# A routed mixture-of-experts kernel on one core: TensorE's branches, its flags, and the place of one transposition in the step

## The chip, the cores and the metric

The kernel runs on one core of a Trainium2 chip. Five engines work beside each other, each through its own list of instructions in the order of the program: TensorE (PE, matrix products; PEld are its weight loads), VectorE (DVE), ScalarE (ACT), GpSimd (POOL) and SyncE (SP, which here issues the loads of weights). They wait for one another by semaphores. The metric is the device time in microseconds (us) of one execution; the time of a kernel is the median of its runs.

## The reference

Attention with a sigmoid, a two-layer network with PReLU, and then a mixture of eight experts of which each token takes one. The change lies in the last part alone:

```python
logits = x @ w_gate                      # 1792 tokens x 768, 8 experts
expert_idx = np.argmax(logits, axis=1)
gate_w = probs[np.arange(N), expert_idx]
for e in range(E):
    xe = x[expert_idx == e]
    h = np.maximum(xe @ w1[e], 0.0)      # 768 x 1024
    ye = h @ w2[e]                       # 1024 x 768
    out[mask] = gate_w[mask, None] * ye
```

All is float32. Each factor of a product is split into a high part that TensorE takes exactly and a low rest, and three products are summed: hi x hi, hi x lo and lo x hi (the "rests").

## The kernel before

**Blocks.** The tokens of an expert are gathered into blocks of 128 slots. There can be 21 of them (TMAX); how many there are, which expert each has and which tokens, is found on the chip. Here 17 blocks run, 0 to 16. Steps 1 to 13 are laid out one behind the other; from there on a chain of branches (tail) asks before each step whether there is another block. A block with 64 tokens or fewer is "half full": its low parts are put into the free slots 64 to 127 of the high tile, so the hi products do the rests too, and the rests are skipped. Here blocks 2, 12 and 13 are half full. Each engine learns that by itself: hold(b) loads slot 64 of the block's list into a register of PE, ACT and DVE, and full(b) compares it with the number of tiles NT.

**Work of one block b.** tx(b) turns the gathered tokens xg (from block 3 on on DVE: L784, into xt; ACT copies xt into bh, L785; DVE makes the rest bl, L786). moe1(b) on PE: 24 hi products of bh with the high (L797) and low (L798) parts of w1, then 12 rests of bl (L806) behind a branch (L810). ACT copies the sum into hr (L814). th(b): eight 128x128 transpositions of hr on PE (L840), then hh on ACT and hl on DVE. moe2(b) on PE: 32 hi products (L894, L895) and 16 rests (L897). out_rows(b) scales the rows on DVE (ye, L911; a half-full block also uses ACT), and POOL scatters them.

**The step.** The whole program is recorded in the order in which the code is run (a manual schedule): no scheduler moves anything. step(b) runs: out_rows and scatter of block b-2; the split of w2 for block b-1, if its expert is new (ACT L700, DVE L701, eight pieces each), and the next load of w2 on SP; moe1(b); the gathers for block b+2 on POOL; tx(b+1); the split of w1 for block b+1, if its expert is new (ACT L679, DVE L681 and L684), and the next load of w1; moe2(b-1), with th(b) put in ahead of its last two rounds of products. So every engine finds work of three blocks in its list. moe1(1) has tx(2), and moe1(2) has th(1), at a place between: behind its hi products. Experts change at blocks 3, 4, 6, 13 and 14: w2 is split in steps 4, 5, 7, 14 and 15, w1 in steps 2, 3, 5, 12 and 13.

**Places.** In the trace of before, moe1(4) starts on PE at about 683 us of the span, moe1(5) at 701, moe1(6) at 719, moe1(9) at 771, moe1(13) at 840, moe1(14) at 855, moe1(15) at 872.

Of the kernel before, what the change touches and what calls it, by code (L numbers as in the profile page):

```python
# [20 lines left out]
ACT = mybir.EngineType.Activation  # L21
DVE = mybir.EngineType.DVE
PE = mybir.EngineType.PE
# [3 lines left out]
def kernel(ctx, tc, kq, v, w_in, w_out, alpha, w_gate, w1, w2, out):  # L27
# [13 lines left out]
    nc = tc.nc  # L41
    P = 128
# [4 lines left out]
    NT, DM = out.shape  # L47
    HP = DM // P
    NF = w_in.shape[0]
    E, _, _, F2 = w1.shape  # L50
    K2 = F2 // P
    HN = DM // 2
    NTT = NT // P
    TMAX = (NT + E * (P - 1)) // P
# [354 lines left out]
    rt = {}  # L409
# [233 lines left out]
    ex = {}  # L643
# [101 lines left out]
    def ps2(key, name):  # L745

        if "fix" not in ex:
            return psum2(name)
        if key not in fixed:
            fixed[key] = psum2(f"f{key}")  # L750
        return fixed[key]

    H = P // 2
    HALF = 2
    held = {}

    def full(b):

        return held[b] < NT

    def hold(b):
        if b >= HALF:
            held[b] = nc.values_load(rt["ids"][H:H + 1, b:b + 1], engines=[PE, ACT, DVE], min_val=0, max_val=2 * 4096)

    def tx(b):

        xg = ex["xg"][b % 4]
        bh, bl = ex["bx"][b % 2]
        hold(b)
        if b < 3:  # L770
            pt = ps2("x", f"tx{b}")
            for k in range(HP):
                nc.tensor.transpose(pt[:, k // 4, (k % 4) * P:(k % 4 + 1) * P], xg.rearrange("p (r k) -> p k r", k=HP)[:, k, :], ident)
            parts = [(pt[:, z, :n * P].rearrange("p (k m) -> p k m", k=n), slice(4 * z, 4 * z + n)) for z, n in ((0, 4), (1, 2))]
            for src, d in parts:
                nc.scalar.activation(bh[:, d, :], src, AF.Copy)
            for src, d in parts:
                nc.vector.tensor_tensor(bl[:, d, :], src, bh[:, d, :].bitcast(F32), ALU.subtract)
        else:

            if "xt" not in ex:
                ex["xt"] = main.tile([P, HP, P], F32, tag="raw", bufs=2, name="xt")
            t = ex["xt"]
            nc.vector.transpose(t.rearrange("p k (q s) -> p k q s", q=G), xg.rearrange("p (q i k) -> p k q i", q=G, k=HP))  # L784
            nc.scalar.activation(bh, t, AF.Copy)  # L785
            nc.vector.tensor_tensor(bl, t, bh.bitcast(F32), ALU.subtract)  # L786
        if b >= HALF:
            with tc.If(held[b] >= NT):  # L788
                nc.vector.tensor_copy(bh[:, :, H:], bl[:, :, :H].bitcast(F32))

    def moe1(b, between=None):
        bh, bl = ex["bx"][b % 2]
        pt = ps2("2" if b == 1 else "1", f"e1_{b}")
        for k in range(HP):
            _, _, h, l = ex["w1"][k]
            for n in range(2):
                nc.tensor.matmul(pt[:, n, :], bh[:, k, :], h[n], start=(k == 0), stop=False)  # L797
                nc.tensor.matmul(pt[:, n, :], bh[:, k, :], l[n], start=False, stop=(b >= HALF and k == HP - 1))  # L798
        if between:
            between()  # L800

        def rests():
            for k in range(HP):
                h = ex["w1"][k][2]
                for n in range(2):
                    nc.tensor.matmul(pt[:, n, :], bl[:, k, :], h[n], start=False, stop=(k == HP - 1), skip_group_check=b >= HALF)  # L806
        if b < HALF:
            rests()
        else:
            with tc.If(full(b)):  # L810
                rests()
        if b == 1:
            next_split(1, 2)
        nc.scalar.activation(ex["hr"], pt, AF.Relu if b < HALF else AF.Copy)  # L814
# [15 lines left out]
    def turn(b, n):  # L830

        if "fix" not in ex:
            pt = psum1(f"th{b}_{n}")
        else:
            if f"t{n}" not in fixed:
                fixed[f"t{n}"] = psum1(f"ft{n}")
            pt = fixed[f"t{n}"]
        for k in range(4):
            sl = slice(k * P, (k + 1) * P)
            nc.tensor.transpose(pt[:, sl], ex["hr"][:, n, sl], ident)  # L840
        return pt

    def turned(b, n, pt):
        hh, hl = ex["hh"][b % 2][:, n, :], ex["hl"][b % 2][:, n, :]
        nc.scalar.activation(hh, pt, AF.Copy)
        nc.vector.tensor_tensor(hl, pt, hh.bitcast(F32), ALU.subtract)
# [20 lines left out]
    def th(b, halves=(0, 1)):  # L867
        if b < HALF:
            for n in halves:
                turned(b, n, turn(b, n))  # L870
        else:
            turned_pair(b, [turn(b, n) for n in range(2)])
# [14 lines left out]
    def moe2_mm(b, pt, k, n, parts="hl", end=False):  # L887

        ks = slice((k % 4) * P, (k % 4 + 1) * P)
        a, c = (ex[x][b % 2][:, k // 4, ks] for x in ("hh", "hl"))  # L890
        h, l = ex["w2"][k]
        ns = slice(n * HN, (n + 1) * HN)
        if "h" in parts:
            nc.tensor.matmul(pt[:, n, :HN], a, h[:, ns], start=(k == 0), stop=False)  # L894
            nc.tensor.matmul(pt[:, n, :HN], a, l[:, ns], start=False, stop=end)  # L895
        if "l" in parts:
            nc.tensor.matmul(pt[:, n, :HN], c, h[:, ns], start=False, stop=(k == K2 - 1), skip_group_check=b >= HALF)  # L897

# [23 lines left out]
    def moe2(b, between):  # L922
        pt = ps2("2", f"e2_{b}")
        for k in range(K2):
            if k == K2 - 2:
                between()
            for n in range(2):
                moe2_mm(b, pt, k, n, "h", b >= HALF and k == K2 - 1)

        def rests():  # L930
            for k in range(K2):
                for n in range(2):
                    moe2_mm(b, pt, k, n, "l")
        if b < HALF:
            rests()
        else:
            with tc.If(full(b)):
                rests()

        def store():  # L940
            out_rows(b, ex["y"][b % 2].rearrange("p (a n) -> p a n", a=2), pt[:, :, :HN])
            scatter(b)
        ex["store"] = store

    def stored():
        ex.pop("store", lambda: None)()
# [14 lines left out]
    def moe2_last(b):  # L961

        next_split(2, b)
        stored()
        hh, hl = ex["hh"][b % 2], ex["hl"][b % 2]
        y = ex["y"][b % 2]
        TH = DM // 3
        for n, (c0, c1) in enumerate(((0, 2 * TH), (2 * TH, DM))):
            pt = ps2("1x"[n], f"e2_{b}_{n}")[:, 0, :]
            for k in range(K2):  # L970
                ks = slice((k % 4) * P, (k % 4 + 1) * P)
                x = hh[:, k // 4, ks]
                h, l = (w[:, c0:c1] for w in ex["w2"][k])
                nc.tensor.matmul(pt[:, :c1 - c0], x, h, start=(k == 0), stop=False)
                nc.tensor.matmul(pt[:, :c1 - c0], x, l, start=False, stop=(k == K2 - 1))
            with tc.If(full(b)):
                for k in range(K2):
                    xl, h = hl[:, k // 4, (k % 4) * P:(k % 4 + 1) * P], ex["w2"][k][0][:, c0:c1]
                    nc.tensor.matmul(pt[:, :c1 - c0], xl, h, start=False, stop=(k == K2 - 1), skip_group_check=True)
            out_rows(b, y[:, c0:c1], pt[:, :c1 - c0])  # L980
            for z in range(c0 // TH, c1 // TH):
                scatter(b, z)
# [13 lines left out]
    def next_split(which, b):  # L996
        if b < TMAX:
            c = (nc.values_load(rt["row0"][0:1, 2:3], engines=[ACT, DVE], min_val=0, max_val=1)
                 if (which, b) == (1, 1) else changed(b, [ACT, DVE]))
            with tc.If(c > 0):  # L1000
                for k in range(HP if which == 1 else K2):
                    (split_w1 if which == 1 else split_w2)(k)

    def second_weights(b):
        next_split(2, b)
        next_w(2, b + 1)

    def step(b, s2=None):
        for _ in s2 or ():
            pass  # L1010
        stored()
        if b > 1:
            second_weights(b - 1)
        moe1(b, {1: lambda: tx(2), 2: lambda: th(1)}.get(b))
        gate_of(b)
        if b + 2 < TMAX:
            gather(b + 2)
        if 1 < b < TMAX - 1:
            tx(b + 1)
        if b > 1:  # L1020
            next_split(1, b + 1)
        next_w(1, b + 2)
        if b > 1:
            moe2(b - 1, lambda: th(b))
# [18 lines left out]
    with tc.manual_schedule():  # L1043
# [12 lines left out]
        c0, c1 = NCH - 2, NCH - 1  # L1056
# [87 lines left out]
        pt = turn(0, 1)  # L1144
# [82 lines left out]
```

## Time and profile before

| | before |
|---|---|
| median of 3 runs | 935.57 us (935.48 to 935.58) |
| the profiled execution | 930.77 us |
| its span in the profile | 929.0 us |
| mean granted clock of TensorE in it | 0.993 of full speed |
| PE busy | 907.8 us, 98% of the span |
| DVE, ACT busy | 566.3 us (61%), 346.4 us (37%) |
| mixture of experts | about 640 to 929 us of the span |

The profile is of one execution. Times in it count from the start of its span. Its summary gives the busy time of each engine and its share; a list of waits says for each engine which producer's instruction ended its idle time ("PE f L894 <- ACT hr L814" is: PE, about to run line 894, waited for ACT's write of hr in line 814); a name with q (DVEq, PEldq) is the engine's instruction queue, as against its arithmetic. A timeline gives single instructions or runs of them with start and length, and in brackets the idle time ahead of the first with what ended it. The granted clock is the share of full speed (2.4 GHz) that TensorE was given; 0.50 is 1.2 GHz.

### The profile page before, as it was taken

How to read it: one execution, taken by the hardware profiler on the slowest of the kernel's cores; microseconds unless marked ns; L12 is line 12 of the kernel's file. 1: busy time of each engine (PE TensorE's matmuls, PEld its weight loads, DVE VectorE, ACT ScalarE, POOL GpSimd, SP SyncE). 2: the span in 40 equal slices, each digit the busy share in tenths (PEclk: the TensorE clock that was granted, in tenths of full speed). 3: DMA queues.
4: the chain of work that ended last, by engine and by line, in shares of the span. 5: the costliest groups of instructions: out<-in, count | busy, mean ns of one | idle time of the engine just before them, and what ended most of it. 6: DMA issues, size and time to landing. Idle time of an engine off the chain costs nothing. (4 is left out here: it accounts for less than half of the span.)

```text
span 929.0 us, 14602 instructions
## 1 busy us (share of the span) xinstructions
PE 907.8 (98%) x5367; PEld 753.6 (81%) x5367; DVE 566.3 (61%) x1017; ACT 346.4 (37%) x543; POOL 137.9 (15%) x149
## 2 busy tenths in 40 slices
PE   9999999999999999999999999999999999999895
PEld 3333348989999899998999899988888899888795
DVE  2765534467777677776777644685588632247831
ACT  6666642222232222322223232343476421144710
POOL 0000000000000000000000000137254442433531
PEclk9999999999999999999999999999999999999898
DMA  7665500011121111211112021451667511148400
GB/s 274 189 202 177 182 1 1 1 52 52 52 68 52 52 52 52 69 52 52 52 52 68 18 85 53 154 238 47 248 248 291 186 52 35 44 171 306 156 19 33
DMA packets 28011, 97.15 MB, mean 105 GB/s; under 512 B 7691, under 2 KB 8441, under 8 KB 24848
## 3 DMA queue, kind: packets, MB, share of 16 engines
q1 hardware_dynamic: 22640, 84.98, 27.1%
q0 software_dynamic: 5280, 11.04, 3.5%
q8 instruction: 47, 0.77, 0.4%
q14 instruction: 44, 0.36, 0.1%
HBM read 162.44 MB, written 12.20 MB: 188 GB/s over the span
## 5 line engine op out<-in xcount | busy, mean ns | idle before, releaser
L388 PE MATMUL y<-wo,gh 128*128 128x384 f32 x448 | 150.8, 337 | 0.0
L390 PE MATMUL y<-wo,gl 128*128 128x384 f32 x448 | 150.0, 335 | 0.0
L389 PE MATMUL y<-wo,gh 128*128 128x384 f32 x448 | 149.9, 335 | 0.0
L395 DVE TENSOR_TENSOR acc<-y,acc 128x768 f32<-128x768 f32 x98 | 93.0, 950 | 14.8 <-PE y L390 14.8
L364 ACT ACTIVATE r<-h 128x512 f32<-128x512 f32 (+1 forms) x64 | 34.8, 544 | 166.0 <-PE h L362 166.0
L366 DVE SCALAR_TENSOR_TENSOR t<-r,alpha,t 128x512 f32<-128x512 f32 (+1 forms) x64 | 43.8, 684 | 83.8 <-ACT t L365 83.8
L388 PEld LDWEIGHTS y<-wo,gh 128*128 128x128 f32 x448 | 84.2, 188 | 1.3 <-issue 0.4
L389 PEld LDWEIGHTS y<-wo,gh 128*128 128x128 f32 x448 | 84.2, 188 | 0.9
L709 POOL MEMSET xg<- 128x768 f32 x4 | 2.8, 742 | 548.9 <-PE xt L433 548.9
L390 PEld LDWEIGHTS y<-wo,gl 128*128 128x128 f32 x448 | 84.1, 188 | 0.0
L242 ACT ACTIVATE a<-sc,bias 128x896 f32<-128x896 f32 x72 | 67.3, 1006 | 36.8 <-PE sc L251 36.7
L797 PE MATMUL f<-w_b,bh 128*128 128x512 f32 x192 | 77.0, 401 | 3.5 <-DVEq L788 2.2
L728 POOL DMA_INDIRECT xg<-x2d,rt_qids x64 | 72.7, 1136 | 19.5 <-issue 17.4
L362 PE MATMUL h<-xa,wi 128*128 128x512 f32 x192 | 75.0, 391 | 0.0
L361 PE MATMUL h<-xa,wi 128*128 128x512 f32 x192 | 74.9, 390 | 0.0
L360 PE MATMUL h<-xa,wi 128*128 128x512 f32 x192 | 74.8, 390 | 0.0
L368 DVE TENSOR_TENSOR gl<-t,gh 128x512 fp32r<-128x512 f32 (+1 forms) x64 | 40.0, 625 | 41.3 <-ACT gh L367 41.3
L894 PE MATMUL f<-w,hh 128*128 128x384 f32 x180 | 60.6, 337 | 4.4 <-ACT hr L814 3.2
L362 PE MATMUL h<-xb,wi 128*128 128x512 f32 (+1 forms) x192 | 64.6, 337 | 0.0
L361 PE MATMUL h<-xb,wi 128*128 128x512 f32 (+1 forms) x192 | 64.6, 337 | 0.0
L360 PE MATMUL h<-xb,wi 128*128 128x512 f32 (+1 forms) x192 | 64.5, 336 | 0.0
L895 PE MATMUL f<-w,hh 128*128 128x384 f32 x180 | 61.1, 339 | 0.0
(270 smaller groups left out, 1729.7 us busy)
## 6 DMA issues: line engine op xcount, KB each, us to landing
raw_e<-in_w_dram SPq DMA_DIRECT2D x72, 1536.0 KB
raw_i<-in_w_in_dram SPq DMA_DIRECT2D x32, 384.0 KB
raw_o<-in_w_out_dram SPq DMA_DIRECT2D x32, 384.0 KB
kq_raw<-in_kq_dram SPq DMA_DIRECT2D x24, 448.0 KB
v<-in_v_dram SPq DMA_DIRECT2D x12, 448.0 KB
x2d<-acc SPq DMA_DIRECT2D x14, 384.0 KB
xg<-x2d,rt_qids POOLq DMA_INDIRECT x64, 3.0
out_dram<-ye,rt_ids POOLq DMA_INDIRECT x18, 3.1
```

The costliest lines, as they stand in the source:

```text
L242: nc.scalar.activation(a, pt[:, :, :S], AF.Sigmoid, bias=bias, scale=scale)
L360: nc.tensor.matmul(pt[:, :n], wh[:, ks], a, start=(k == 0), stop=False)
L361: nc.tensor.matmul(pt[:, :n], wh[:, ks], b, start=False, stop=False)
L362: nc.tensor.matmul(pt[:, :n], wl[:, ks], a, start=False, stop=(k == HP - 1))
L388: nc.tensor.matmul(pt[:, nh, :HN], gh[:, j, ts], wh[:, ns], start=(j == 0), stop=False)
L389: nc.tensor.matmul(pt[:, nh, :HN], gh[:, j, ts], wl[:, ns], start=False, stop=False)
L390: nc.tensor.matmul(pt[:, nh, :HN], gl[:, j, ts], wh[:, ns], start=False, stop=(j == 1))
L395: nc.vector.tensor_tensor(dst, pt[:, :, :HN], dst, ALU.add)
L728: nc.gpsimd.indirect_dma_start(out=dst, out_offset=None, in_=src, in_offset=at, bounds_check=src.shape[0] - 1, oob_is_err=False)
L797: nc.tensor.matmul(pt[:, n, :], bh[:, k, :], h[n], start=(k == 0), stop=False)
L894: nc.tensor.matmul(pt[:, n, :HN], a, h[:, ns], start=(k == 0), stop=False)
L895: nc.tensor.matmul(pt[:, n, :HN], a, l[:, ns], start=False, stop=end)
```

## The change

Three things change.

First, at the three places where PE skips the rests of a half-full block (moe1, moe2, moe2_last), the last hi x lo product is held back and written into both arms of the branch: the arm with the rests begins with it, and the other arm, which was empty, consists of it.

Second, the register with slot 64 is loaded under two names, one for PE and one for ACT and DVE. A branch on the first is in PE's program alone, a branch on the second in those of ACT and DVE alone.

Third, tx(b+1) is written ahead of moe1(b) from step 3 on (in step 2 it stays behind it), and what moe1(1) and moe1(2) have in between (tx(2), th(1)) moves from behind their hi products to the middle of them.

```diff
@@ -754,13 +754,15 @@
     HALF = 2
     held = {}
 
-    def full(b):
-
-        return held[b] < NT
+    def full(b, engines="av"):
+
+
+        return held[engines, b] < NT
 
     def hold(b):
         if b >= HALF:
-            held[b] = nc.values_load(rt["ids"][H:H + 1, b:b + 1], engines=[PE, ACT, DVE], min_val=0, max_val=2 * 4096)
+            for k, engines in (("pe", [PE]), ("av", [ACT, DVE])):
+                held[k, b] = nc.values_load(rt["ids"][H:H + 1, b:b + 1], engines=engines, min_val=0, max_val=2 * 4096)
 
     def tx(b):
 
@@ -785,30 +787,37 @@
             nc.scalar.activation(bh, t, AF.Copy)
             nc.vector.tensor_tensor(bl, t, bh.bitcast(F32), ALU.subtract)
         if b >= HALF:
-            with tc.If(held[b] >= NT):
+            with tc.If(held["av", b] >= NT):
                 nc.vector.tensor_copy(bh[:, :, H:], bl[:, :, :H].bitcast(F32))
 
     def moe1(b, between=None):
         bh, bl = ex["bx"][b % 2]
         pt = ps2("2" if b == 1 else "1", f"e1_{b}")
         for k in range(HP):
+            if k == HP // 2 and between:
+                between()
             _, _, h, l = ex["w1"][k]
             for n in range(2):
                 nc.tensor.matmul(pt[:, n, :], bh[:, k, :], h[n], start=(k == 0), stop=False)
-                nc.tensor.matmul(pt[:, n, :], bh[:, k, :], l[n], start=False, stop=(b >= HALF and k == HP - 1))
-        if between:
-            between()
+                if b < HALF or (k, n) != (HP - 1, 1):
+                    nc.tensor.matmul(pt[:, n, :], bh[:, k, :], l[n], start=False, stop=(b >= HALF and k == HP - 1))
 
         def rests():
             for k in range(HP):
                 h = ex["w1"][k][2]
                 for n in range(2):
                     nc.tensor.matmul(pt[:, n, :], bl[:, k, :], h[n], start=False, stop=(k == HP - 1), skip_group_check=b >= HALF)
+
+        def last():
+            nc.tensor.matmul(pt[:, 1, :], bh[:, HP - 1, :], ex["w1"][HP - 1][3][1], start=False, stop=True)
         if b < HALF:
             rests()
         else:
-            with tc.If(full(b)):
+            with tc.If(full(b, "pe")) as cmp:
+                last()
                 rests()
+            with cmp.Else():
+                last()
         if b == 1:
             next_split(1, 2)
         nc.scalar.activation(ex["hr"], pt, AF.Relu if b < HALF else AF.Copy)
@@ -892,7 +901,10 @@
         ns = slice(n * HN, (n + 1) * HN)
         if "h" in parts:
             nc.tensor.matmul(pt[:, n, :HN], a, h[:, ns], start=(k == 0), stop=False)
-            nc.tensor.matmul(pt[:, n, :HN], a, l[:, ns], start=False, stop=end)
+            if not end:
+                nc.tensor.matmul(pt[:, n, :HN], a, l[:, ns], start=False, stop=b >= HALF and k == K2 - 1)
+        if "z" in parts:
+            nc.tensor.matmul(pt[:, n, :HN], a, l[:, ns], start=False, stop=True)
         if "l" in parts:
             nc.tensor.matmul(pt[:, n, :HN], c, h[:, ns], start=False, stop=(k == K2 - 1), skip_group_check=b >= HALF)
 
@@ -925,7 +937,7 @@
             if k == K2 - 2:
                 between()
             for n in range(2):
-                moe2_mm(b, pt, k, n, "h", b >= HALF and k == K2 - 1)
+                moe2_mm(b, pt, k, n, "h", b >= HALF and (k, n) == (K2 - 1, 1))
 
         def rests():
             for k in range(K2):
@@ -934,8 +946,11 @@
         if b < HALF:
             rests()
         else:
-            with tc.If(full(b)):
+            with tc.If(full(b, "pe")) as cmp:
+                moe2_mm(b, pt, K2 - 1, 1, "z")
                 rests()
+            with cmp.Else():
+                moe2_mm(b, pt, K2 - 1, 1, "z")
 
         def store():
             out_rows(b, ex["y"][b % 2].rearrange("p (a n) -> p a n", a=2), pt[:, :, :HN])
@@ -972,11 +987,15 @@
                 x = hh[:, k // 4, ks]
                 h, l = (w[:, c0:c1] for w in ex["w2"][k])
                 nc.tensor.matmul(pt[:, :c1 - c0], x, h, start=(k == 0), stop=False)
-                nc.tensor.matmul(pt[:, :c1 - c0], x, l, start=False, stop=(k == K2 - 1))
-            with tc.If(full(b)):
+                if k < K2 - 1:
+                    nc.tensor.matmul(pt[:, :c1 - c0], x, l, start=False, stop=False)
+            with tc.If(full(b, "pe")) as cmp:
+                nc.tensor.matmul(pt[:, :c1 - c0], x, l, start=False, stop=True)
                 for k in range(K2):
-                    xl, h = hl[:, k // 4, (k % 4) * P:(k % 4 + 1) * P], ex["w2"][k][0][:, c0:c1]
-                    nc.tensor.matmul(pt[:, :c1 - c0], xl, h, start=False, stop=(k == K2 - 1), skip_group_check=True)
+                    xl, wh = hl[:, k // 4, (k % 4) * P:(k % 4 + 1) * P], ex["w2"][k][0][:, c0:c1]
+                    nc.tensor.matmul(pt[:, :c1 - c0], xl, wh, start=False, stop=(k == K2 - 1), skip_group_check=True)
+            with cmp.Else():
+                nc.tensor.matmul(pt[:, :c1 - c0], x, l, start=False, stop=True)
             out_rows(b, y[:, c0:c1], pt[:, :c1 - c0])
             for z in range(c0 // TH, c1 // TH):
                 scatter(b, z)
@@ -1011,12 +1030,14 @@
         stored()
         if b > 1:
             second_weights(b - 1)
+        if 2 < b < TMAX - 1:
+            tx(b + 1)
         moe1(b, {1: lambda: tx(2), 2: lambda: th(1)}.get(b))
         gate_of(b)
         if b + 2 < TMAX:
             gather(b + 2)
-        if 1 < b < TMAX - 1:
-            tx(b + 1)
+        if b == 2:
+            tx(3)
         if b > 1:
             next_split(1, b + 1)
         next_w(1, b + 2)
```

The first place is the end of moe1 on PE, here that of moe1(3). f is the sum of the first layer, w_b and w_c the parts of w1, bh and bl the tokens, hh the turned hidden rows. The last line is the first product of moe2. Before:

```order
L798 MATMUL f_6058<-w_c_5283,bh_5618 128x512 [waits DVE_49]
L810 COMPARE_AND_BRANCH
L806 MATMUL f_6058<-w_b,bl_5619 128x512 x12
L810 UNCONDITIONAL_BRANCH
L810 UNCONDITIONAL_BRANCH [waits PE_49]
L763 TENSOR_LOAD rt_ids
L763 ISA x2
L788 COMPARE_AND_BRANCH
L788 UNCONDITIONAL_BRANCH x2
L894 MATMUL f_5881<-w_0_5418,hh_5429 128x384 [waits DVE_49,Activation_49]
```

After:

```order
L801 MATMUL f_6067<-w_b,bh_5618 128x512
L816 COMPARE_AND_BRANCH
L812 MATMUL f_6067<-w_c_5283,bh_5618 128x512 [waits DVE_49]
L809 MATMUL f_6067<-w_b,bl_5619 128x512 x12
L816 UNCONDITIONAL_BRANCH
L812 MATMUL f_6067<-w_c_5283,bh_5618 128x512 [waits DVE_49]
L816 UNCONDITIONAL_BRANCH
L903 MATMUL f_5881<-w_0_5418,hh_5429 128x384 [waits DVE_49,Activation_49]
```

The empty arm, which waited for PE's own semaphore (PE_49), has become an arm with one product; the load of the next block's slot 64 (L763) and the branch on it (L788) no longer stand here (the load stands ahead of moe1).

The second place is ACT in a step, here step 4. w2h is the high part of w2 (the split's last two of eight pieces), bh the tokens of block 5, hr the hidden rows of block 4. Before:

```order
L700 ACTIVATE w2h_5424<-raw_e 128x768
L700 ACTIVATE w2h_5426<-raw_e 128x768
L1000 UNCONDITIONAL_BRANCH x2
L810 COMPARE_AND_BRANCH
L810 UNCONDITIONAL_BRANCH x2
L814 ACTIVATE hr<-f_6058 128x1024
L763 TENSOR_LOAD rt_ids
L785 ACTIVATE bh_5150<-xt 128x768
L788 COMPARE_AND_BRANCH
```

After:

```order
L700 ACTIVATE w2h_5424<-raw_e 128x768
L700 ACTIVATE w2h_5426<-raw_e 128x768
L1019 UNCONDITIONAL_BRANCH x2
L765 TENSOR_LOAD rt_ids
L765 ISA x2
L787 ACTIVATE bh_5150<-xt 128x768
L790 COMPARE_AND_BRANCH
L790 UNCONDITIONAL_BRANCH x2
L823 ACTIVATE hr<-f_6067 128x1024
```

hr has moved behind bh of the next block; PE's branch (L810) has left ACT's list.

The third place is PE in moe1(2), where th(1) stands (ft: the two halves of the turned rows). Before:

```order
L798 MATMUL f_6058<-w_c_5283,bh_5150 128x512 [waits DVE_49]
L840 MATMUL ft_6083<-ident,hr 128x128 [waits Activation_49]
L840 MATMUL ft_6083<-ident,hr 128x128 x3
L840 MATMUL ft_6090<-ident,hr 128x128 x4
L810 COMPARE_AND_BRANCH
```

After:

```order
L803 MATMUL f_6067<-w_b,bh_5150 128x512
L849 MATMUL ft_6080<-ident,hr 128x128 [waits Activation_49]
L849 MATMUL ft_6080<-ident,hr 128x128 x3
L849 MATMUL ft_6087<-ident,hr 128x128 x4
L801 MATMUL f_6067<-w_b,bh_5150 128x512
L803 MATMUL f_6067<-w_c_5282,bh_5150 128x512 [waits DVE_49]
```

The transpositions have moved ahead of the second half of the hi products.

## Rows read from the trace of the kernel before

**Rows 1.** Summary of the page: busy us (share of the span) and instructions, by engine.

```profile
PE 907.8 (98%) x5367; PEld 753.6 (81%) x5367; DVE 566.3 (61%) x1017; ACT 346.4 (37%) x543; POOL 137.9 (15%) x149
```

**Rows 2.** Waits of PE, 640 to 930 us, by releaser: total us, times, longest.

```profile
PE f L894 <- ACT hr L814: 3.2, 2, 1.7
...
PE f L894 <- ACT hh L845: 1.3, 1, 1.3
...
PE f L797 <- DVE w_c L684: 0.7, 1, 0.7
PE f L797 <- PE f L895: 0.6, 1, 0.6
```

**Rows 3.** Stretches: length, busy by engine (instructions), granted clock, DMA share, GB/s.

```profile
700.85:718.93 18.08, 17.67 (x93) 15.88 (x93) 15.25 (x17) 13.47 (x17) 7.28 (x6) 1.00 0.73 283
718.93:736.38 17.45, 17.45 (x93) 15.97 (x93) 9.54 (x13) 6.51 (x10) 6.69 (x6) 1.00 0.60 219
771.25:776.73 5.48, 5.48 (x26) 4.50 (x25) 2.63 (x2) 0.00 (x0) 2.79 (x3) 1.00 0.18 72
783.63:785.92 2.29, 2.29 (x17) 2.28 (x16) 0.88 (x2) 1.09 (x2) 0.00 (x0) 1.00 0.03 7
873.31:879.01 5.70, 5.70 (x13) 4.51 (x14) 5.44 (x8) 4.78 (x7) 1.48 (x2) 0.50 0.37 148
```

**Rows 4.** PE's queue, 823 to 848 us: duration ns min/median/max, first and last start.

```profile
L810 PEldq COMPARE_BRANCH  x2: 208/208/208, 825.0 to 841.7; - x2
L810 PEldq EVENT_SEMAPHORE  x2: 51/51/51, 829.2 to 845.9; - x2
...
L763 PEldq TENSOR_LOAD <-rt_ids x2: 303/392/480, 829.6 to 846.1; - x2
```

**Rows 5.** Timeline of PE: start us, length us, instruction, idle before it.

```profile
695.80 1.04 PE L840 MATMUL ft<-ident,hr 128*128 128x128 f32 x8
...
830.93 0.41 PE L894 MATMUL f<-w,hh 128*128 128x384 f32 x1 [1.73 <-ACT hr L814]
...
847.34 0.41 PE L894 MATMUL f<-w,hh 128*128 128x384 f32 x1 [1.43 <-ACT hr L814]
...
872.17 0.77 PE L797 MATMUL f<-w_b,bh 128*128 128x512 f32 x1 [2.22 <-DVEq L788]
...
873.31 0.80 PE L798 MATMUL f<-w_b,bh 128*128 128x512 f32 x1 [0.38 <-DVEq L1000]
```

**Rows 6.** Timeline of ACT in step 4.

```profile
691.91 1.03 ACT L814 ACTIVATE hr<-f 128x1024 f32<-128x1024 f32 x1
698.42 0.85 ACT L785 ACTIVATE bh<-xt 128x768 fp32r<-128x768 f32 x1 [5.48 <-DVE xt L784]
```

**Rows 7.** Timeline of DVE from step 2 to step 4.

```profile
657.08 1.29 DVE L846 TENSOR_TENSOR hl<-ft,hh 128x512 fp32r<-128x512 f32 x2 [7.36 <-ACT hh L845]
658.61 1.63 DVE L784 STREAM_TRANSPOSE xt<-xg 128x768 f32<-128x768 f32 x1 [0.23 <-issue]
...
689.80 5.31 DVE L701 TENSOR_TENSOR w<-raw_e,w 128x768 fp32r<-128x768 f32 x6
...
696.77 1.61 DVE L784 STREAM_TRANSPOSE xt<-xg 128x768 f32<-128x768 f32 x1
```

**Rows 8.** Timeline of ACT in steps 12 and 14.

```profile
829.39 1.02 ACT L814 ACTIVATE hr<-f 128x1024 f32<-128x1024 f32 x1 [9.09 <-PEq L810]
830.32 0.83 ACT L785 ACTIVATE bh<-xt 128x768 fp32r<-128x768 f32 x1
831.05 5.80 ACT L679 ACTIVATE w_b<-raw_e 128x1024 fp32r<-128x1024 f32 x6
...
870.13 0.84 ACT L785 ACTIVATE bh<-xt 128x768 fp32r<-128x768 f32 x1 [3.14 <-DVE xt L784]
```

**Rows 9.** Timeline of DVE in step 12.

```profile
825.97 1.62 DVE L784 STREAM_TRANSPOSE xt<-xg 128x768 f32<-128x768 f32 x1 [1.13 <-issue]
...
833.18 3.50 DVE L681 TENSOR_TENSOR w_b<-raw_e,w_b 128x1024 fp32r<-128x1024 f32 x3 [0.58 <-ACT w_b L679]
```

## The prediction

> **What bounds the kernel now.** I read the busy shares first [rows 1]: PE is busy 907.8 of 929.0 us, so it sets the time as long as nobody makes it wait. All edits lie in the mixture-of-experts part (640 to 929 us), so next came PE's waits there by what ended them [rows 2], and the longest of them in PE's order of time [rows 5]. Then the stretches [rows 3]. A step with a full block and nothing in the way takes 17.45 us with PE busy throughout (the second stretch); the step of block 5 takes 18.08 (the first). The 24 hi products of a first layer take 5.48, or 0.228 each (the third); the eight turns of th and the eight products behind them 2.29 (the fourth). The fifth stretch is out of line: the 13 products from 873.31 took 5.70 at a granted clock of 0.50 (1.2 GHz). At 0.228 each they are 2.97, so 2.73 us went to the clock, right behind an idle of 2.22 and one of 0.38 [rows 5].
>
> So the time is PE's work, plus its waits, plus what the clock takes after a long one. The profiled execution took 930.77 us (its span 929.0), 4.80 below the median 935.57; my sum is a difference on its span, put on the median.
>
> **Part 1: the arms that end with a product, and the flags.** Where a block is half full, PE skips the rests, and the skipping arm waits for PE's own products before it goes on (first order piece of the change). In steps 12 and 13 that costs 1.73 and 1.43 [rows 5], the 3.2 of rows 2: the compare ran at 825.0, the EVENT_SEMAPHORE at 829.2, then came a load of 303 to 480 ns, and ACT could take hr only after that [rows 4, 8]. The wait at 829.2 thus stands 4.2 us behind its compare: the sequencer runs that far ahead of the products, and this hides its loads and branches in the full blocks, where moving or sharing them costs or gives 0 (17.45 us with PE busy all of it [rows 3]). Bounds for the branches: the three compares that PE no longer makes in a step would give 3 x 208 ns if they stood bare [rows 4], and as much would be lost if the arms' new jumps did; the step of 17.45 has no place for either. I take 0. The gain is then the waits themselves: 1.73, 1.43, and 0.6 at the start of step 4, where moe2(2) of a half-full block ends [rows 2]. The 0.7 at step 14 is PE waiting for DVE's w1 split [rows 2]; it goes only if DVE comes earlier.
>
> **Part 2: th(1) half a first layer earlier.** In step 2 PE waits 1.3 for hh(1) [rows 2]. With th(1) after 12 of the 24 products, hh(1) and hl(1) come 12 x 0.228 = 2.74 us sooner. PE gains 1.3. DVE gains more: it sat idle for 7.36 until hl(1) at 657.08 and took xt(3) at 658.61 right behind; the splits for two experts follow, up to xt(5) [rows 7]. So its chain and ACT's can come up to 2.74 sooner. Bounds: 0 (if the gathered tokens or the weights of the next expert arrive no sooner) to 2.74; I take 2.74, since the long rest ahead of hl(1) ended with ACT's hh and not with a transfer [rows 7].
>
> **Part 3: tx(b+1) ahead of moe1(b).** On DVE nothing changes places: moe1 has no DVE work, and xt(b+1) still stands behind the w2 split L701. No DMA moves; the gather on POOL and the loads on SP stand where they stood. The change is on ACT (second order piece): hr(b), the copy that PE's th(b) needs, now stands **behind** bh(b+1), which waits for DVE. In a step without a w2 split xt is early and this costs nothing. In a step with one (steps 4, 5, 7, 14, 15) it is a new wait on PE's path. Step by step:
>
> Step 4. Before, hr(4) was copied at 691.91, well ahead of th(4) at 695.80 [rows 5, 6]. bh(5) ran at 698.42, after an idle of 5.48, because xt(5) came behind the w2 split [rows 6, 7]. In the new order hr(4) ends at 698.42 + 0.85 + 1.03 = 700.30; less the 2.74 of part 2 that is 697.56, and th(4) is 1.76 **later** than before. PE, with 1.3 and 0.6 gained, would be there at about 693.9 and idles some 3.7. So the gains of steps 2 and 3 are swallowed. Step 5 then finds DVE less behind and runs in 17.45, not 18.08: -0.63. Net +1.13.
>
> The clock in step 4. An idle of 3.7 is longer than the 2.22 and 0.38 [rows 5] behind which the granted clock fell to 0.50 [rows 3]. Bounds: 0 (no fall) to the one priced fall, 2.73. I take 2.73, for the nearest row is a shorter idle that had it.
>
> Step 14. Before, bh(15) ran at 870.13 [rows 8]; hr(14) now ends at 870.13 + 0.84 + 1.03 = 872.00, less what the chain is earlier. In step 12 xt(13) was done at 825.97 + 1.62 = 827.59, but bh(13) had to stand behind hr(12) until 830.32 [rows 8, 9]; it now goes first, and the w1 split of block 13 starts on DVE when hr(12) (829.39 + 1.02 = 830.41) and the first of six w1 copies (5.80 / 6 = 0.97) are done, 831.4 for 833.18: 1.8 sooner. Of this 0.4 goes back in step 13, where hr(13) is behind bh(14): 1.4. So hr(14) is there at 870.6, and moe1(15) starts 2.29 later [rows 3], at 872.9. Before, it began at 872.17 but had to stop behind one product [rows 5]; without that stop it would have begun at 873.31 - 0.23 = 873.1. That is -0.2; the stretch at 1.2 GHz comes here as before, over somewhat more work: the 2.29 of th and its products lie in it as well, of which I take a sixth, +0.4 (bounds 0 and 2.29). Net +0.2. The gaps of steps 12, 13 and 14 that PE may no longer have (1.73 + 1.43 + 0.7) end in a longer wait for hr(14) and give nothing.
>
> Steps 5, 7 and 15 have a w2 split too, but no w1 split in the step ahead, which in steps 4 and 14 still holds DVE when the step begins. Bounds for each: 0 to the length of one xt, 1.61 [rows 7], by which hr could come late; I take 0.
>
> **Sum.** 1.13 + 2.73 + 0.2 = +4.1: 935.57 + 4.06 = 939.6. The profiled execution would be 934.8.
>
> **A rule beside it.** What the trace shows of ACT's order: bh(13) stood 2.7 us behind hr(12) although its input was there [rows 8, 9]. The Trainium skill, "TensorE: Matmul & The Clock Gate", section "Architectural detail: the array is 16× 32×32, not 1× 128×128", says that the queues of VectorE and ScalarE are strictly first in, first out, while TensorE's may pull weight loads ahead. By that rule the faster rival below has no way round its wait; the trace agrees with those 2.7 us. If ACT could pass, the sum would be that rival's.
>
> **Rivals.**
> Faster: hr(4) and hr(14) are not late, either since ACT's chain comes over 4.5 us sooner (700.30 - 4.5 = 695.8) or since ACT takes hr first. Then PE gains its five gaps, 1.3 + 0.6 + 1.73 + 1.43 + 0.7 = 5.8, and the time is 929.8; with the stop at 872 and its clock gone too (2.6 + 2.73), 924.5. For it: each gap is real and part 1 and part 2 aim at them. Against: the order on ACT is fixed, and the most that part 2 can move is 2.74. Chance 0.10.
> The clock holds: the idle of step 4 is not followed by a fall. 939.6 - 2.73 = 936.9, within 0.2%. For it: rows 3 show only one fall. Chance 0.15.
> The chain is not earlier: DVE is held by a gather or a load of weights, and hr(4) comes at 700.30. It adds 2.74: 942.4. Chance 0.12.
> The arms do nothing: the product in the arm still waits (it names DVE in its wait) and steps 12 and 13 keep their gaps. As DVE's chain decides at step 14, the sum hardly moves: 939.6 to 940.3. Chance 0.03.
>
> **How the numbers follow.** Forecast 0.60, and the rivals as given. Two per mille, 1.9 us, is about what a measurement tells from no change: same is 933.7 to 937.4. Slower: 0.60 + 0.12 + 0.03 = 0.75; same 0.15; faster 0.10. The range takes in the clock that holds (936.9, less 0.5 for its size) and the chain that is not earlier (942.4, plus half an xt, 0.8, for the steps held at 0): 936.4 to 943.2, and leaves out the faster rival and a little beyond each end.
>
> **What would show it.** Right: in step 4 and in step 14 PE waits 3 us or more for ACT's hr ahead of th; on ACT bh waits for DVE's xt with hr behind it; the granted clock falls to 0.50 behind step 4's wait; the gaps of PE in steps 2, 12 and 13 are gone. Wrong: th(4) no later than before against the start of moe1(4), or full speed behind it, or gaps that stay where a block is half full. If the time is below 933, step 14's wait is the term that I have wrong, as it holds the most gaps.

## The result, and the profile after

The changed kernel takes 941.27 us (median of five runs, 939.75 to 941.67), the kernel before 935.48 beside it (five runs, 932.50 to 935.58): slower by the ratio 1.0065 (95% interval 1.0048 to 1.0083), or 5.8 us. Forecast were +4.1 us and 939.6. On two other chips (below) the same two kernels differ by less: 933.62 against 930.24, ratio 1.0036 (1.0021 to 1.0052), and 933.60 against 930.15, ratio 1.0041 (1.0026 to 1.0056). All three are slower and clear of no change; what differs between them comes below, under "What I didn't see".

The summary and the waits of PE (line that waits, releaser, total us, times, longest) of the changed kernel's profiled execution, 941.42 us with a span of 939.5. Its lines are those of the new file: hr is L823 (was L814), bh L787 (L785), xt L786 (L784), th L849 (L840), moe1 L801, L803, L812 (L797, L798), moe2 L903, L905 (L894, L895), hh(1) L854 (L845). In the lines of the profile f is the sum of a layer and ft the turned rows; an x with a number counts instructions.

```profile
PE 912.7 (97%) x5367; PEld 757.3 (81%) x5367; DVE 566.9 (60%) x1017; ACT 346.5 (37%) x543; POOL 135.2 (14%) x149
...
PE ft L849 <- ACTq L1019: 8.7, 2, 4.4
PE f L903 <- ACT hh L854: 4.3, 1, 4.3
PE f L903 <- DVE ye L932: 1.3, 1, 1.3
```

Against [rows 2] the list has turned over. The gaps behind half-full blocks (hr, 3.2 in two; the 0.6 at the start of step 4) and the 2.2 ahead of moe1(15) are gone. In their place PE waits twice for hr ahead of th: 8.7 us in two waits. A third one, 4.3 for hh(1) in step 2, nobody had forecast. PE's busy time has grown by 4.9 us over [rows 1] with the same 5367 products. Most of that is the clock: by its mean, 0.989 of 939.5 us against 0.993 of 929.0, an estimate of 3.8 us.

The two places of the forecast, on PE's timeline and on ACT's (start us, length, instruction, idle ahead of it with its releaser):

```profile
705.10 1.97 PE L849 MATMUL ft<-ident,hr 128*128 128x128 f32 x8 [4.37 <-ACTq L1019]
...
881.39 1.97 PE L849 MATMUL ft<-ident,hr 128*128 128x128 f32 x8 [4.30 <-ACTq L1019]
```

```profile
703.16 0.84 ACT L787 ACTIVATE bh<-xt 128x768 fp32r<-128x768 f32 x1 [4.96 <-DVE xt L786]
704.02 1.02 ACT L823 ACTIVATE hr<-f 128x1024 f32<-128x1024 f32 x1
```

bh(5) waits 4.96 for DVE's xt; hr(4) runs right behind it and ends at 705.04; th(4) begins at 705.10. The eight turns take 1.97 in place of 1.04 [rows 5]. The releaser that the profile names (ACTq L1019) is ACT's queue; the last thing that ACT wrote for th is hr. The stretches behind both waits (columns as in [rows 3]: length, busy, granted clock third from the end):

```profile
705.10:709.60 4.50, 4.50 (x17) 4.50 (x18) 1.39 (x2) 1.19 (x2) 0.00 (x0) 0.50 0.98 391
881.39:886.90 5.51, 5.51 (x19) 5.32 (x20) 1.49 (x3) 2.11 (x4) 0.00 (x0) 0.50 0.55 222
```

Both run at 0.50, 1.2 GHz, as the stretch from 873.31 did before [rows 3].

### The profile page after: what moved, and what is told of

Same layout as the page of the kernel before. It is cut to its first block, busy times and chain, and to the rows that moved or that the text cites. A ratio compares the mean times of both kernels' runs of the same rounds, so it can differ in the third digit from the quotient of the medians.

```text
span 939.5 us, 14446 instructions
## 1 busy us (share of the span) xinstructions
PE 912.7 (97%) x5367; PEld 757.3 (81%) x5367; DVE 566.9 (60%) x1017; ACT 346.5 (37%) x543; POOL 135.2 (14%) x149
## 5 line engine op out<-in xcount | busy, mean ns | idle before, releaser
L801 PE MATMUL f<-w_b,bh 128*128 128x512 f32 x192 | 75.7, 394 | 0.0
L728 POOL DMA_INDIRECT xg<-x2d,rt_qids x64 | 70.1, 1095 | 19.5 <-issue 17.4
L903 PE MATMUL f<-w,hh 128*128 128x384 f32 x180 | 61.4, 341 | 5.7 <-ACT hh L854 4.3
L905 PE MATMUL f<-w,hh 128*128 128x384 f32 x180 | 62.8, 349 | 0.6 <-DVE w L701 0.6
```

Of the source, the lines that this page charges most:

```text
L728: nc.gpsimd.indirect_dma_start(out=dst, out_offset=None, in_=src, in_offset=at, bounds_check=src.shape[0] - 1, oob_is_err=False)
```

## The experiments

Theory A is that of the prediction: the loss lies in steps 4 and 14, where hr now stands behind bh, and in the clock behind these waits. Theory B grew out of the profile above: the wait of 4.34 us for hh(1) in step 2 belongs to the change and is the loss. C and D are rivals for single parts and stand in the expectations (C of the run with the flags alone is another one than C of the run with the arms alone). The twelve runs fell on three chips, four on each; each is compared with the kernel before on its own chip, which took 930.15 to 930.29 on all three.

### The kernel before, again

> The kernel before, unchanged, for a second profile. Its profiled execution (930.77 us) was 4.8 us below its median, that of the changed kernel was not, so the spans of the two profiles (929.0 and 939.5) differ by 10.5 us where the medians differ by 5.8. Theory A (the loss is in steps 4 and 14, by the copy hr behind bh): median 935.5, ratio 1.000; a second profile, if it is near the median, shows some 4 to 5 us more than the first one in one place that has nothing to do with the change. Theory B (the 4.34 us for which TensorE waits in step 2 of the changed kernel, for hh(1), belong to the change): no execution of the kernel before has such a wait; step 2's wait for hh stays at 1.3.

Measured: 930.63 (before beside it 930.29; ratio 1.000, 0.9990 to 1.0009). The wait for hh(1) is 1.26, as in [rows 2]. The 935.5 that I expected did not come. The rows of the first profile repeat within half a us up to th(14), so that profile (930.77 us) is a usual one, near the median of this chip. The 4.8 us that I set it below the median belong to the first chip's runs, of which I have no trace of the kernel before.

### tx back behind moe1

> The changed kernel with tx(b+1) put back behind moe1(b) in all steps; the arms, the flags and the middle place of th(1) stay. Theory A: the waits for hr in steps 4 and 14 (4.37 and 4.30 us) and the slow clock behind step 4 go: 941.3 - 6.6 in steps 4 and 5, and the gaps of the arms (1.73, 1.43) stay away: 930 to 935. Theory B: the loss is in step 2 and stays: 939 to 941.

```diff
-        if 2 < b < TMAX - 1:
-            tx(b + 1)
         moe1(b, {1: lambda: tx(2), 2: lambda: th(1)}.get(b))
...
-        if b == 2:
-            tx(3)
+        if 1 < b < TMAX - 1:
+            tx(b + 1)
```

Measured: 926.85 against 930.29, ratio 0.9964 (0.9949 to 0.9979): faster than both kernels (the 930 to 935 that I expected were on the level of the first chip). The waits for hr are gone, step 4 runs at full clock, and step 2 has no wait for hh at all. What is left is step 14, where DVE is late for moe1(15) as before, with the granted clock at 0.50 behind it; PE's two longest waits:

```profile
PE f L801 <- DVEq L790: 2.2, 1, 2.2
PE f L903 <- DVE ye L932: 1.3, 1, 1.3
```

So the moved tx (part 3 of the prediction) costs the time, and the arms, the flags and the middle place together bring some: theory A. Theory B falls, since all of the change that runs up to step 2 is in this kernel.

### tx ahead alone

> The kernel before with tx(b+1) ahead of moe1(b) from step 3 on, and nothing else. Theory A: th(4) comes 700.30 - 695.80 = 4.5 us later, the clock behind that wait takes 2.7, step 5 gives 0.6 back: 935.5 + 6.6 = 942.1, and up to 1.5 more in step 14; a slow stretch of the clock behind th(4). Theory B: within 1 us of 935.5.

```diff
+        if 2 < b < TMAX - 1:
+            tx(b + 1)
         moe1(b, {1: lambda: tx(2), 2: lambda: th(1)}.get(b))
...
-        if 1 < b < TMAX - 1:
-            tx(b + 1)
+        if b == 2:
+            tx(3)
```

Measured: 937.65 against 930.29, ratio 1.0076 (1.0056 to 1.0095), +7.4; expected +6.6 and up to 1.5 more. PE's and ACT's timelines, and the stretch behind the first wait:

```profile
700.09 1.97 PE L840 MATMUL ft<-ident,hr 128*128 128x128 f32 x8 [3.69 <-ACTq L1000]
...
876.56 1.97 PE L840 MATMUL ft<-ident,hr 128*128 128x128 f32 x8 [4.30 <-ACTq L1000]
```

```profile
698.14 0.84 ACT L785 ACTIVATE bh<-xt 128x768 fp32r<-128x768 f32 x1 [6.26 <-DVE xt L784]
699.01 1.02 ACT L814 ACTIVATE hr<-f 128x1024 f32<-128x1024 f32 x1
```

```profile
700.09:705.30 5.21, 5.21 (x19) 5.21 (x20) 1.38 (x2) 1.19 (x2) 0.00 (x0) 0.50 1.00 395
```

hr(4) ends at 700.03. The prediction had put it at 700.30 from [rows 6] without any gain from the other parts. The clock falls behind an idle of 3.69, and 5.21 us at half speed are 2.6 lost. Steps 4 and 14 also begin 1.53 and 1.67 late behind DVE's w1 split (0.56 and 0.70 in the kernel before), which I had not counted; the changed kernel has no such waits.

### th(1) in the middle, alone

> The kernel before with tx(2) and th(1) in the middle of the hi products of moe1(1) and moe1(2), and nothing else. Theory A: the wait of 1.3 us for hh(1) goes, and since DVE's chain comes up to 2.7 us sooner nothing new is late: 932.5 to 935.5. Theory B: a wait of some 4 us for hh(1) in step 2 as in the changed kernel: 938 to 940.

```diff
         for k in range(HP):
+            if k == HP // 2 and between:
+                between()
...
-        if between:
-            between()
```

Measured: 930.11 against 930.29, ratio 1.000 (0.9986 to 1.0014). Nothing comes of it, and both halves of its reckoning were off. PE still stops for 1.26 us ahead of moe2(1), although hh(1) is done 3.5 us sooner:

```profile
657.36 0.44 PE L893 MATMUL f<-w,hh 128*128 128x384 f32 x1 [1.26 <-ACT hr L813]
```

What ends there is the skipping arm of half-full block 2, the same wait as in steps 12 and 13; in [rows 2] it stood under hh's name, whose write happened to come last. (With the arms alone, below, it is gone.) And the chain comes less far ahead than th(1) does. ACT's w1 split, then DVE's xt(3) and xt(5):

```profile
659.71 2.96 ACT L679 ACTIVATE w_b<-raw_e 128x1024 fp32r<-128x1024 f32 x3 [1.67 <-DMA raw_e<-in_w_dram]
664.19 2.96 ACT L679 ACTIVATE w_b<-raw_e 128x1024 fp32r<-128x1024 f32 x3 [1.52 <-DMA raw_e<-in_w_dram]
```

```profile
655.12 1.57 DVE L784 STREAM_TRANSPOSE xt<-xg 128x768 f32<-128x768 f32 x1 [0.24 <-issue]
...
695.68 1.61 DVE L784 STREAM_TRANSPOSE xt<-xg 128x768 f32<-128x768 f32 x1
```

xt(3) is 3.5 us ahead of [rows 7], xt(5) only 1.1: the split now waits twice for the weights of block 3, which SP loads when it did before.

### The changed kernel, again

> The changed kernel, unchanged, beside the three kernels below and for a second profile. Theory A (steps 4 and 14): ratio 1.006 as before, and the wait of 4.34 us for hh(1) in step 2, which the changed kernel without the moved tx did not show, is gone here as well; th(4) comes some 3 us later than in the kernel before (4.5 less the 1.2 by which xt(5) came sooner in the run with the middle place alone). Theory B (step 2's wait belongs to the change as a whole): the wait of 4 us is there again.

Measured: 933.62 against 930.24, ratio 1.0036. Step 2's wait is not there. All of PE's waits of this second profile (933.60 us, span 931.7):

```profile
PE ft L849 <- ACTq L1019: 9.3, 3, 4.4
PE f L903 <- DVE ye L932: 1.2, 1, 1.2
PE f L905 <- DVE w L701: 0.7, 2, 0.4
PE f L989 <- DVEq L1019: 0.7, 1, 0.7
```

Its places, to be set beside [rows 5]:

```profile
697.94 1.97 PE L849 MATMUL ft<-ident,hr 128*128 128x128 f32 x8 [4.37 <-ACTq L1019]
...
874.20 1.97 PE L849 MATMUL ft<-ident,hr 128*128 128x128 f32 x8 [4.31 <-ACTq L1019]
...
891.24 1.10 PE L849 MATMUL ft<-ident,hr 128*128 128x128 f32 x8 [0.59 <-ACTq L1019]
```

```profile
697.94:703.30 5.36, 5.36 (x20) 5.36 (x21) 1.39 (x2) 1.30 (x3) 0.00 (x0) 0.50 1.01 391
...
717.99:735.44 17.45, 17.45 (x94) 15.97 (x93) 11.84 (x14) 7.75 (x10) 5.65 (x6) 1.00 0.40 140
874.20:877.50 3.30, 3.30 (x13) 3.30 (x14) 1.36 (x2) 1.19 (x2) 0.00 (x0) 0.50 0.91 376
```

th(4) is 2.14 later than in [rows 5] (3 was expected here, 1.76 in the prediction). But moe1(1), which starts ahead of all that was moved, does so at 640.00 here and at 640.87 in the profile of [rows 5]; the third profile of the changed kernel has 641.30, so this is no work of the change. Counted from moe1(1), th(4) is 3.0 later. th(5) at 717.99 is 4.1 later than the 713.89 of the kernel before (5.0 from moe1(1)); between th(5) and th(6) lie 17.45 us without a wait, and the shift stays at 4.1 until the half-full blocks. Steps 12 and 13 give back 3.6 (th(13) stands 0.46 later than before), and th(14) takes 6.2. As the stop of 2.22 and 0.38 ahead of moe1(15) [rows 5] is gone and the slow stretch is 3.30 long and not 5.70 [rows 3], th(15) is 3.0 later and the end of the span 2.7.

### The arms alone

> The kernel before with the arms that end with a product, and nothing else (one flag for all engines, tx behind moe1, th(1) at the end). Theory A: the gaps behind skipped rests go (1.3 in step 2, which I take for PE's own wait now and not for hh, 0.6, 1.73, 1.43), and DVE's chain in step 14 takes some of that back: 2.0 to 3.5 us faster than before. Rival C (the sequencer hides all branches, the gaps are the copies of hr and not the skipping arm): within 0.5 us of before.

The edit is the first part of the change, with one flag for all engines. Measured: 929.58 against 930.24, ratio 0.9991 (0.9978 to 1.0004): 0.7 faster by the medians and not clear of no change, below the 2.0 to 3.5 that I expected. The gaps did go, that of step 2 too, with th(1) at its old place. th(13) stands at 848.44 in place of 851.60, 3.2 sooner; but th(14) at 868.11 in place of 867.52 is later, and then moe1(15) stops as before:

```profile
861.44 0.41 PE L903 MATMUL f<-w,hh 128*128 128x384 f32 x1 [1.40 <-DVE ye L932]
...
871.88 0.47 PE L798 MATMUL f<-w_b,bh 128*128 128x512 f32 x1 [1.33 <-DVEq L789]
873.02 0.50 PE L800 MATMUL f<-w_b,bh 128*128 128x512 f32 x1 [0.67 <-DVEq L1019]
```

These are new or kept waits for DVE in step 14: it takes back what steps 12 and 13 gave. About half of that is the clock: behind the 1.40, and a further 0.41 at 862.26, it was 0.50 from 864 to 866. moe1(15) starts at 871.88 where it started at 872.17 [rows 5], although th(13) was 3.2 sooner. Rival C falls (the gaps were the skipping arm's), and that DVE's chain decides when moe1(15) starts is shown without the moved tx.

### The changed kernel without the middle

> The changed kernel with tx(2) and th(1) back behind the hi products; arms, flags and the moved tx stay. Theory A: xt(5) and with it hr(4) come 1.2 us later than in the changed kernel, as the weights of block 3 held the split: 1.2 slower than it, ratio to before 1.007 to 1.008. Rival D (the middle place gives its whole 2.74): 2.7 slower than the changed kernel, ratio 1.009.

Measured: 935.07, 1.45 above the changed kernel beside it (933.62), ratio to before 1.0054 (1.0039 to 1.0070). The ratio is below the 1.007 to 1.008 that theory A named, as the changed kernel's own ratio fell to 1.0036; the difference of 1.45 is near theory A's 1.2 and not rival D's 2.7. So in the changed kernel the middle place is worth half of its 2.74. th(4) begins at 699.33, 1.4 later than with the middle, but 0.9 of that is the start of moe1(1), at 640.89 here.

### tx still further ahead

> The changed kernel with tx(b+1) put still further ahead, to the start of the step, in front of the rows and the w2 split of block b-1. Theory A: bh(b+1) no longer waits for the split, so neither hr(4) nor hr(14) is late and moe1(15) finds bh ready (no stop of 2.2 and no slow clock behind it); DVE does xt and bl (2.6 us) ahead of the split, so moe2(3) and moe2(13) wait some 2.5 each for pieces of w2: 925 to 929 where before is 930.3, about as fast as the changed kernel with tx behind moe1. If hr was not what was late (theory B): as slow as the changed kernel.

```diff
     def step(b, s2=None):
...
+        if 2 < b < TMAX - 1:
+            tx(b + 1)
         stored()
         if b > 1:
             second_weights(b - 1)
-        if 2 < b < TMAX - 1:
-            tx(b + 1)
         moe1(b, {1: lambda: tx(2), 2: lambda: th(1)}.get(b))
```

Measured: 953.37 against 930.24, ratio 1.0252 (1.0233 to 1.0271): 23 us slower, against an expected gain. hr is indeed never late here (no wait of th's is left), but I had not counted when the gathered tokens land. xt now heads DVE's queue and waits for them, with the rows and the splits behind it, for which PE waits in its turn (7.1 us in two waits for the rows, ye):

```profile
DVE xt L786 <- DMA xg<-x2d,rt_qids: 40.2, 10, 7.7
```

It is the changed kernel's fault once more, one place further up: a wait at the head of an in-order queue holds whatever stands behind it.

### Part of the split on GpSimd

> The changed kernel with tx behind moe1 (the faster one of the runs so far), and the low parts of the last two of eight pieces of each w2 split made by GpSimd in place of VectorE. DVE is the engine that is late in step 14: it has 1.81 us less there, so xt(15) comes that much sooner, the stop of 2.2 us ahead of moe1(15) shrinks to 0.4 and the slow clock behind it goes: 3 to 4 us faster than with all pieces on DVE, 922.5 to 924 where before is 930.3. If GpSimd takes over 4 us for the two pieces or waits for its own gathers, moe2(13) waits for them instead: no gain, or a loss of up to 4.

```diff
-        nc.vector.tensor_tensor(l[:, s], src, h[:, s].bitcast(F32), ALU.subtract)
+        (nc.gpsimd if n is None and k >= K2 - 2 else nc.vector).tensor_tensor(l[:, s], src, h[:, s].bitcast(F32), ALU.subtract)
```

Measured: 929.50 against 930.15, ratio 0.9993 (0.9984 to 1.0003): slower than without it (0.9964, on another chip), the outcome that the expectation gives in its last sentence. The stop ahead of moe1(15) shrinks to 0.48, as expected; the profile's mean clock is 0.996, as it was without it. But the two pieces take GpSimd 3.58 and 4.88 us where DVE takes 1.81 for the same two in the kernel before, and moe2(3) waits for them; GpSimd in steps 4 and 14, and PE's wait:

```profile
690.38 3.58 POOL L702 TENSOR_TENSOR w2l<-raw_e,w2h 128x768 fp32r<-128x768 f32 x2
...
868.09 4.88 POOL L702 TENSOR_TENSOR w2l<-raw_e,w2h 128x768 fp32r<-128x768 f32 x2 [1.90 <-ACT w2h L701]
```

```profile
694.83 0.44 PE L906 MATMUL f<-w,hh 128*128 128x384 f32 x1 [3.50 <-DVE w L702]
```

### The flags alone

> The kernel before with own flags for TensorE, and nothing else. Theory A: the sequencer runs some 4 us ahead of the products and hides the compares that PE no longer makes; where a block is half full, PE has one compare less behind its wait: 0 to 0.5 us faster. Rival C: each compare that goes from the bare places (208 ns, up to eight of them) counts: 1.5 us faster.

Measured: 931.92 against 930.15, ratio 1.0021 (1.0011 to 1.0030): slower by 1.8, which neither theory had. Up to th(16) it is ahead, at 902.84 where a profile of the kernel before on the same chip has 904.64; 0.6 of these 1.8 stand there already at moe1(1) (640.63 against 641.26). Then PE stops inside the first products of moe2_last, with nothing to wait for:

```profile
908.92 0.39 PE L976 MATMUL f<-w,hh 128*128 128x512 f32 x1
911.90 0.39 PE L975 MATMUL f<-w,hh 128*128 128x512 f32 x1 [2.59 <-issue]
912.13 0.54 PE L976 MATMUL f<-w,hh 128*128 128x512 f32 x1
912.47 0.63 PE L975 MATMUL f<-w,hh 128*128 128x512 f32 x1
```

"issue" is time in which the profile shows nothing that PE waits for, and the products behind it are slower: the granted clock is 0.50 from 913 to 915. From th(16) to the end are 27.3 us in place of 23.3. The changed kernel has no such stop (23.0 in its second profile). So in this profile the flags by themselves gain some 1.2 us before the tail, where I had taken 0, and lose 4 in it. What the stop is, the profile doesn't show and no run tested.

### Both kernels, a third time

> The changed kernel, a third profile beside the next one. Theory A: ratio to before 1.0036 to 1.0065; without the wait of 4.34 us for hh(1) in step 2 the span is some 932 and the ratio the lower one, with it 939 and the higher one.

> The kernel before, a third profile. If step 2's long wait for hh(1) is a matter of the chip and not of the change, it shows here whenever it shows in the run above (then median 935.5, span 934), and is absent (1.3 us; median 930.3) when it is absent there.

Measured: 933.60 and 930.52, beside 930.15: ratios 1.0041 and 1.0001. Neither has the long wait of step 2; that of the kernel before is 1.16. In this profile of the changed kernel the two waits for hr are again 4.37 and 4.31. These two profiles are the best pair to set beside each other, on one chip and with the same start; first the changed kernel's moe1(1) and th(4), then those of the kernel before:

```profile
641.30 0.39 PE L801 MATMUL f<-w_b,bh 128*128 128x512 f32 x1
...
698.74 1.87 PE L849 MATMUL ft<-ident,hr 128*128 128x128 f32 x8 [4.37 <-ACTq L1019]
```

```profile
641.26 0.39 PE L797 MATMUL f<-w_b,bh 128*128 128x512 f32 x1
...
695.87 1.04 PE L840 MATMUL ft<-ident,hr 128*128 128x128 f32 x8
```

DVE's xt(5), in the same order:

```profile
695.18 1.52 DVE L786 STREAM_TRANSPOSE xt<-xg 128x768 f32<-128x768 f32 x1
```

```profile
696.83 1.61 DVE L784 STREAM_TRANSPOSE xt<-xg 128x768 f32<-128x768 f32 x1
```

th(4) is 2.9 later, th(5) 3.9 (717.87 against 713.98), th(15) 3.2 (890.39 against 887.19), the end of the span 2.9 (930.8 against 927.9).

## Why the prediction was right, point by point

**The sign and the place.** hr behind bh, bh behind xt, xt behind the w2 split: th(4) and th(14) wait, in all three profiles of the changed kernel and with tx ahead alone, and not with tx behind. Idle forecast in step 4: 3.7; measured 4.37, and 3.69 with tx ahead alone.

**Step 4's delay.** 1.76 forecast, 2.9 measured in the third profile, 2.14 in the second (3.0 from its moe1(1)): the term was some 1.1 too small. The wait of 1.3 in step 2 was read as hh's; it was the skipping arm's, and goes all the same, by part 1. What was mis-sized is the chain. I took it to be 2.74 earlier (the upper bound, chosen because the long rest ahead of hl(1) ended with hh). xt(5) starts at 695.18 in the third profile and at 696.83 in the kernel before beside it: 1.6 earlier, since the weights of block 3 were the next thing to be late, the lower bound's reason. 700.30 less 1.6 is 698.7, where hr(4) does end (698.68). The middle place alone gave 1.1, and the shared branches were not quite the 0 that I gave them: DVE rests 1.13 ahead of xt(13) in [rows 9], and 0.94 in the changed kernel's second profile.

**Step 5.** 17.45 without a stop forecast, and found: between th(4) and th(5) of the second profile lie 20.05 us, which is 17.45 and the clock's 2.6.

**The clock in step 4.** +2.73 forecast. 5.36 us at half speed, 2.7 lost, in the second profile; 5.21 in the run with tx ahead alone. In the third only 1.7 are lost: th(4) to th(5) takes 19.13 there, against 17.45. Together, steps 4 and 5: +3.86 forecast; at th(5) +4.1 in the second profile (+5.0 from moe1(1)) and +3.9 in the third. There the sum is met because a delay taken 1.1 too short and a clock taken 1.0 too dear cancel, which is luck.

**Step 14.** hr(14) at 870.6, moved by the 3.86 of steps 4 and 5, is 874.5; th(14) began at 874.20. The gains of steps 12 and 13 are swallowed there, as the run with the arms alone shows too. The net of +0.2 was wrong in its clock: I let the slow stretch be as long as before (5.70), and that fits the first profile (5.51) but not the second (3.30, 1.2 us less lost) and the third (2.7). The measured net from th(5) to th(15) is -1.1 in the second profile and -0.7 in the third. In it is step 15's wait of 0.59, which I held at 0, within its bound of 1.61.

**The sum.** By the second profile against the first one of the kernel before, 4.1 of steps 2 to 5, -1.1 up to th(15) and -0.3 behind it make the 2.7 by which the spans differ; by the third against the kernel before beside it, 3.9, -0.7 and -0.3 make 2.9. The medians on these two chips differ by 3.4, 0.7 under the forecast; on the first chip they differ by 5.8, 1.7 over it. The mechanism and both places were right; that the number came so near is in part luck, of terms that miss either way and of what follows.

**What I didn't see.** Step 2's wait of 4.34 us in the first profile. hh(1) was turned by 654.3 and copied at 660.70. Behind the wait the granted clock was 0.50 too (from 662 to 665), so th(1) to th(2) takes 14.0 us where the third profile has 7.8. In the same stretch SP issued its instructions slowly: its register loads of that stretch took up to 698 ns (260 to 273 in the second profile), and the load of block 3's weights, issued at 651.5 there, went out at 660.60 here. Both queues were slow at once, the two other profiles of the kernel and the run with tx behind have nothing of it, and no trace of the kernel before from that chip is at hand; it, too, took 5 us more there than on the others. Whether the first ratio is higher for this reason stays open, and so does its cause.

**The rivals.** The faster one had no run for it: with tx at the changed kernel's place no profile has hr(4) or hr(14) early (still further ahead it was early, and the kernel 23 us slower), and the order on ACT held each time, as the rule of the Trainium skill that stands beside the sum says (queues of VectorE and ScalarE strictly first in, first out; "TensorE: Matmul & The Clock Gate", section "Architectural detail: the array is 16× 32×32, not 1× 128×128"). "The clock holds" did not come. "The chain is not earlier" came by some 1.1 of its 2.74. "The arms do nothing" is out.

## What to carry to other kernels

A step that is moved ahead in the program moves ahead in every queue that it has an instruction in, so look in each queue at what it is put in front of and at what its first instruction there waits for. Take the step in which the wait is longest, since a place that is free in most steps decides in the few with extra work. And where a gap is taken away, ask at once who is late next: here the next ones (a load of weights; DVE's rows and split, with the clock behind them) took back half of one gain and most of another.

## What the runs showed of the hardware

The clock's fall is not the same in each execution. The kernel before ran on one chip at spans from 926.0 us, with a mean granted clock of 0.998, to 930.5, with 0.993, with nothing else changed; in its third profile the stop ahead of moe1(15) is there as in [rows 5], but only 3.4 us behind it, from 873.6 to 877, ran at 0.50, in place of 5.70. The mean over a stretch around it:

```profile
872.17:877.00 4.83, 4.16 (x10) 3.10 (x11) 3.43 (x5) 4.54 (x8) 0.00 (x0) 0.65 0.62 254
```

It fell behind 1.40 and 0.41 of idle with the arms alone (861.44 above), and not behind 1.34 and 0.41 in the same place with tx behind moe1 (granted clock 1.00 from 861 to 865). A difference of 3 us between two single executions here says nothing on a change. Waits for one producer can stand under the name of another that ends at the same moment: the 1.26 us of step 2 bore hh's name and was PE's own arm, as it showed when hh came sooner and the wait stayed, and when the arm was changed and it went.
